# The second mixing one step later, with a third buffer of mixed blocks

## The chip, the cores and the metric

The kernel runs on one core of a Trainium2 chip. The metric is device time of one execution in microseconds; the kernel before takes 968.75 us (median of three runs, 968.42 to 970.42).

## The reference

Talking-heads attention, then a feed-forward layer. q, k, v have the shape (4, 12, 448, 64): batches, heads, positions, width of a head. The scores of all 12 heads are mixed across heads before the softmax and once more behind it:

```python
scores = scale * q @ k.T                              # per batch and head, 448 x 448
scores = einsum('bhij,hg->bgij', scores, w_pre)       # first mixing, 12 x 12
attn = exp(scores - max_j); attn = attn / (sum_j attn + 1e-9)
attn = einsum('bhij,hg->bgij', attn, w_post)          # second mixing
x = (attn @ v), heads side by side                    # 1792 x 768
out = (s * relu(x @ w_in)**2 + b) @ w_out             # 768 -> 2048 -> 768
```

## The kernel before

The attention is cut into 16 chunks (four per batch, 110 or 118 query rows each) and these into 180 blocks of 10 (or 9) query rows times 12 heads, 120 partitions by 448 keys. One loop over steps s works on several blocks at once; every engine carries out its instructions in the order in which the loop issues them (nothing reorders them later). In step s stand, in this order:

- `relayout(s+5)`: a DMA brings the scores of a block from `S` (rows by heads) to `blk` (120 partitions). `split(s+2)`, GpSimd (L559, L560): high and low part, `hl`, two buffers.
- One piece of a weight conversion for the later layer (VectorE, with one ScalarE copy `mk` in seven pieces), from step 12 (`CONV0`) until seven units are done.
- `normalize(s-1)`: reciprocal of the sum (VectorE L591) and the high half of the normalized block in fp16, `eh` (ScalarE L593), two buffers.
- `evacuate(s-3)`: copies the mixed block `po` from PSUM into the chunk's tile `A` (VectorE L631, in the last chunk ScalarE L629).
- `premix(s)`: the first mixing, three matmuls into a PSUM bank `pm` (L572; three banks in turn, `pm` twice and `px`), the maximum (VectorE L574), exp in place with its sum (ScalarE L579), the sum scaled (ScalarE L583).
- `remainder(s-1)`: low half of `eh` (VectorE L600), the last reader of the bank.
- `postmix(s-2)`: the second mixing, 12 matmuls of 120 columns with `eh` as weights, into `po` (L615; two PSUM buffers).
- What a plan has for the step: transposes of q and k (`prep_q` L460, `prep_k` L438), `av_pair` (attention times v of two heads, 16 matmuls, L513, with ScalarE copies `xs` L527), `qk_pair` (scores of two heads of a later chunk, six matmuls, L485, evacuated into `S` by ScalarE, L495). In most of the loop AV and QK pairs stand in the same steps, every second one, so heavy and light steps alternate.

The plan gives the AV pairs of chunks 0 to 13 fixed steps, the first not before the chunk's last block is evacuated (`w0 = first[ci + 1] + 3`). The pairs of chunks 14 and 15, and 18 pieces of the later layer's first product (`head_piece`, L247), are dealt out to the last steps by costs and due times; six head pieces and the AV pairs of chunk 15 come after the loop. Then three weight units are converted, `x` of the next batch is split (`xg`, L223 and L232), and the feed-forward layer runs (L247, L300) until the end.

Before the loop a tile of ones, `keep`, feeds matmuls that occupy TensorE while the first data arrive. It has a place of its own in the pool of constants. `mk` is one buffer of 1536 bytes per partition in the conversions' pool `cvp`.

Of the kernel before, what the change touches and what calls it, by code (L numbers as in the profile page):

```python
# [11 lines left out]
F16 = mybir.dt.float16  # L12
# [9 lines left out]
def talking_heads_attention__then__act_relu2_kernel(  # L22
# [14 lines left out]
    B, H, S, D = q.shape  # L37
    DM = H * D
    DFF = moe_w_in.shape[1]
    P = 128  # L40
# [7 lines left out]
    BP = BI * H  # L48
    CH = 120
    NKC = DM // P  # L50
# [11 lines left out]
    NCH = len(chunks)  # L62
# [3 lines left out]
    first = []  # L66
# [9 lines left out]
    NB = len(blocks)  # L76
# [9 lines left out]
    cvp = ctx.enter_context(tc.tile_pool(name="cvp", bufs=1))  # L86

    att = ExitStack()
    cst = att.enter_context(tc.tile_pool(name="cst", bufs=1))
    sp = att.enter_context(tc.tile_pool(name="sp", bufs=2))  # L90
    blkp = att.enter_context(tc.tile_pool(name="blkp", bufs=3))
# [90 lines left out]
    def convert_step(upto):  # L182

        if done["run"] is None:
            if done["conv"] >= min(upto, len(units)):
                return False
            done["run"] = conversion(done["conv"])
        try:
            next(done["run"])
        except StopIteration:  # L190
            done["run"] = None
            done["conv"] += 1
        return True
# [35 lines left out]
    def low_parts():  # L229
        while later:  # L230
            o, x, hi = later.pop(0)
            nc.vector.tensor_tensor(out=o, in0=x, in1=hi.bitcast(F32), op=ALU.subtract)  # L232
# [37 lines left out]
    NHEAD = 3  # L270
# [276 lines left out]
    def relayout(t):  # L547
        ci, i0, ni = blocks[t]
        blk = blkp.tile([BP, S], F32, tag="blk", name=f"blk_{t}", bufs=LD)
        nb = first[ci + 1] - first[ci]  # L550
        r = t - first[ci]
        nc.sync.dma_start(blk[:ni * H, :], s_t[ci][r:r + nb * (ni - 1) + 1:nb, :, :])
        blk_t[t] = blk

    def split(t):
        n = blocks[t][2] * H
        blk = blk_t.pop(t)
        hl = blkp.tile([BP, 2, S], F32R, tag="hl", name=f"hl_{t}", bufs=2)
        nc.gpsimd.tensor_scalar(hl[:n, 0, :], blk[:n], 1.0, 0.0, op0=ALU.mult, op1=ALU.add)  # L559
        nc.gpsimd.tensor_tensor(  # L560
            out=hl[:n, 1, :], in0=blk[:n], in1=hl[:n, 0, :].bitcast(F32), op=ALU.subtract
        )
        hl_t[t] = hl
# [23 lines left out]
    def normalize(t):  # L587

        n = blocks[t][2] * H
        e, st = e_t[t]  # L590
        nc.vector.reciprocal(st[:n, 3:4], st[:n, 2:3])  # L591
        eh = blkp.tile([BP, 2, S], F16, tag="eh", name=f"eh_{t}", bufs=2)
        nc.scalar.activation(eh[:n, 0, :], e[:n], AF.Copy, scale=st[:n, 3:4])  # L593
        eh_t[t] = eh

    def remainder(t):
        n = blocks[t][2] * H
        e, st = e_t.pop(t)
        eh = eh_t[t]
        nc.vector.scalar_tensor_tensor(  # L600
            out=eh[:n, 1, :], in0=e[:n], scalar=st[:n, 3:4], in1=eh[:n, 0, :],
            op0=ALU.mult, op1=ALU.subtract,
        )

    def postmix(t):
        ci, i0, ni = blocks[t]
        n = ni * H
        eh = eh_t.pop(t)
        if i0 == 0:
            a_t[ci] = ap_.tile([P, NC, H, CH], F32, tag="A", name=f"A_{ci}")  # L610
        po = ps.tile([P, 512], F32, tag="po", name=f"po_{t}", bufs=2)
        for c in range(NC):
            j0 = min(c * P, S - P)
            for m, (x, y) in enumerate(((1, 0), (0, 1), (0, 0))):
                nc.tensor.matmul(  # L615
                    po[:, c * BP:(c + 1) * BP],
                    eh[:n, x, j0:j0 + P],
                    wpost[:n, y].rearrange("p g i -> p (g i)"),
                    start=(m == 0),
                    stop=(m == 2),  # L620
                )
        po_t[t] = po

    def evacuate(t):
        ci, i0, ni = blocks[t]
        dst = a_t[ci][:, :, :, i0:i0 + ni]
        src = po_t.pop(t)[:, :NC * BP].rearrange("p (c g i) -> p c g i", c=NC, g=H)[:, :, :, :ni]
        if ci == NCH - 1:
            nc.scalar.activation(dst, src, AF.Copy)  # L629
        else:  # L630
            nc.vector.tensor_copy(dst, src)  # L631
# [3 lines left out]
    FILL = 1.33  # L635
    QK_COST, AV_COST = 0.8, 1.3
    LATE = 6
# [6 lines left out]
    def at(step, order, f, *args):  # L644
        plan.append((step, order, len(plan), f, args))
# [6 lines left out]
    def visits(ci):  # L652

        w0, w1 = first[ci - 1] - LD, first[ci] - LD
        return [w0 + i for i in (1, 3, 5, 7, 9, w1 - w0 - 1)]

    fill = []
    for ci in range(2, NCH):
        b, _, _ = chunks[ci]
        w0 = first[ci - 1] - LD  # L660
# [10 lines left out]
        for p, step in enumerate(visits(ci)):  # L671
            if news:
                t = w0 - back + 8 if p == 0 else w0 + 2 * p - 2
# [4 lines left out]
            load[step] = load.get(step, 0) + QK_COST  # L678
    for ci in range(NCH):
        b = chunks[ci][0]  # L680
        w0 = first[ci + 1] + 3
        if ci < NCH - 2:
            after = visits(ci + 3) if ci + 3 < NCH else [first[NCH - 1] - LD + i for i in (1, 3, 5, 7)]
            steps = [x for x in visits(ci + 2) if x >= w0] + [x for x in after if x < first[ci + 2] + 3]
            assert len(steps) == NP
            for p, step in enumerate(steps):
                at(step, 2, av_pair, ci, p)
                load[step] = load.get(step, 0) + AV_COST
                if b + 1 < B and chunks[ci + 1][0] != b:
                    at(step, 4, load_v, b + 1, p)  # L690
            continue
        w1 = first[ci + 2] + 3 if ci + 2 <= NCH else NB + 100
        if ci == NCH - 1:
            w0 = NB + 3
        for p in range(NP):
            when = w0 + p * min(w1 - w0, 12) / NP
            fill.append((when, w0, w1 - 1, AV_COST, 1, av_pair, (ci, p)))
    w0 = first[NCH - 1] - XA + 2
    for i in range(NHEAD * NKC):
        if i < NHEAD * NKC - LATE:  # L700
            when = w0 + i * (NB + 3 - w0) / (NHEAD * NKC - LATE)
            fill.append((when, w0 + i // 2, NB + 2, 0.567, 1, head_piece, ()))
        else:
            fill.append((NB + 100, NB + 3, NB + 100, 0.567, 1, head_piece, ()))
    fill.sort(key=lambda x: x[0])
    spent, closed = 0.0, {}
    for s in range(NB + 4):
        spent = max(spent, -0.4) + load.get(s, 0)
        left, held = [], set()
        for x in fill:  # L710
            _, lo, hi, cost, order, f, args = x
            waits = f in held

            opens = f is qk_pair or (f is av_pair and args[1] % 4 == 0)
            if opens and closed.get(f, -1) >= s and s <= NB + 2 and s < hi:
                waits = True

            if f is qk_pair and s in load and s < hi:
                waits = True
            if not waits and lo <= s and (s > NB + 2 or hi <= s or (x[0] < s + 4 and spent < FILL)):  # L720
                at(s, order, f, *args)
                spent += cost
                if f is qk_pair or (f is av_pair and args[1] in (3, NP - 1)):
                    closed[f] = s
            else:
                held.add(f)
                left.append(x)
        fill = left
        spent -= FILL
# [12 lines left out]
        if not early:  # L742
            state["next"] = k0

    keep = cst.tile([P, 512], F16, name="keep")
    nc.gpsimd.memset(keep, 1.0)
    make_identity(nc, ident)
    busy = ps.tile([P, 512], F32, tag="px", name="busy")
# [51 lines left out]
    while plan[0][0] < 0:  # L800
        x = plan.pop(0)
        x[3](*x[4])
        low_parts()
    tail = first[NCH - 1]
    for s in range(NB + 3):
        if s == tail - LD:
            early.close()
            rp = ctx.enter_context(tc.tile_pool(name="rp", bufs=1, side="right", reuse_waits="tile"))
            for n in range(NU_EARLY, NU_EARLY + NU_TAIL):
                w_pool[n] = rp  # L810
        if s + LD < NB:
            relayout(s + LD)
        if s + LS < NB:
            split(s + LS)
        if 0 <= s - 1 < NB:
            if s >= CONV0:
                convert_step(NU_EARLY)
            normalize(s - 1)
        if 0 <= s - 3 < NB:
            evacuate(s - 3)  # L820
        if s <= tail - XA:
            low_parts()
        if s < NB:
            premix(s)
        low_parts()
        if 0 <= s - 1 < NB:
            remainder(s - 1)
        run_plan(s, True)
        if 0 <= s - 2 < NB:
            postmix(s - 2)  # L830
        run_plan(s, False)
        if 0 <= s - (tail - LD) < NKC // 2:
            for kc in range(2):
                load_x(0, 0, 2 * (s - (tail - LD)) + kc)
        if 0 <= s - (tail - XA) < NKC:
            split_x(0, 0, s - (tail - XA))
        if 0 <= s - tail < NKC:
            load_x(0, 1, s - tail)
# [106 lines left out]
```

## Time and profile before

| | |
|---|---|
| median of three runs | 968.75 us |
| the profiled execution | 969.14 us, of which the span is 967.4 us |
| TensorE matmul / weight load busy | 928.9 us (96%) / 786.4 us (81%) |
| VectorE / ScalarE / GpSimd busy | 640.2 / 595.8 / 397.1 us |
| the block loop | premix from 30 us to 486 us |

The span runs from the first to the last instruction. PE is TensorE's matmul row, PEld its weight loads, DVE VectorE, ACT ScalarE, POOL GpSimd. The ends of matmuls are modelled and matmuls are pipelined: the start of one after the start of another tells the pace better than their lengths. An idle time in brackets is what the engine sat through before that instruction, and what released it. Names are the program's, with buffer numbers left out.

### The profile page before, as it was taken

The numbers are of one execution on the slowest core, as the hardware profiler recorded it, in microseconds if no ns is written. First come the engines' busy times: TensorE is split into PE (matmuls) and PEld (weight loads), VectorE is DVE, ScalarE is ACT, GpSimd is POOL, SyncE is SP. The second block draws the span as 40 slices with busy tenths as digits, with TensorE's granted clock in tenths as the row PEclk, the third lists the DMA queues.
The fourth block names the chain that finished last, engine by engine and source line by source line (L and its number), as shares of the span: only waits on it lengthen the run. The fifth ranks groups of instructions, "written<-read, shape, count | busy, mean of one in ns | idle before, by whom it ended". The sixth has DMA issues, their size and how long they took to land.

```text
span 967.4 us, 19864 instructions
## 1 busy us (share of the span) xinstructions
PE 928.9 (96%) x7515; PEld 786.4 (81%) x7515; DVE 640.2 (66%) x1314; ACT 595.8 (62%) x1315; POOL 397.1 (41%) x469
## 2 busy tenths in 40 slices
PE   6889999999999999999989999999999999999998
PEld 3656767777777777777779999999998999999998
DVE  4789999888878888788678217746716811849311
ACT  3587777777888888888777878422216787711000
POOL 3766667666676667666613323100001332310000
PEclk8899999999999999999999999999999999999999
DMA  4665645654455544645422302234431410237431
GB/s 103 165 152 143 173 115 147 174 135 136 122 138 145 134 129 116 154 123 160 121 70 90 123 23 84 82 115 139 147 139 42 154 59 1 69 112 215 144 99 50
DMA packets 124252, 114.63 MB, mean 118 GB/s; under 512 B 61656, under 2 KB 120044, under 8 KB 124156
## 3 DMA queue, kind: packets, MB, share of 16 engines
q1 hardware_dynamic: 114630, 101.69, 38.1%
q10 hardware_dynamic: 9366, 11.59, 3.4%
q8 instruction: 59, 0.97, 0.4%
q0 software_dynamic: 160, 0.09, 0.1%
q14 instruction: 37, 0.30, 0.1%
HBM read 58.28 MB, written 16.52 MB: 77 GB/s over the span
## 4 chain that ended last, share of the span: by engine, by line
PE 65%; ACT 14%; DVE 14%; DMA 4%; issue 2%; POOL 1%; SPq 0%; ACTq 0%; DVEq 0%; POOLq 0%
PE po L300 24%; PE ph L247 16%; PE po L615 6%; PE pm L572 5%; PE xp L513 5%; PE sc L485 5%; ACT S L495 4%; ACT pm L579 3%; DVE eh L600 3%; ACT eh L593 3%; DVE A L631 2%; DVE st L574 2%; DMA nq<-in_q_dram 1%; PE trk L438 1%; DMA blk<-S 1%
## 5 line engine op out<-in xcount | busy, mean ns | idle before, releaser
L300 PE MATMUL po<-w,g 128*128 128x384 f32 x1344 | 234.6, 336 | 2.6 <-ACT h L255 2.6
L300 PEld LDWEIGHTS po<-w,g 128*128 128x128 f32 x1344 | 233.7, 188 | 3.3 <-ACT h L255 3.2
L560 POOL TENSOR_TENSOR hl<-blk,hl 120x448 fp32r<-120x448 f32 x180 | 205.8, 1143 | 15.0
L265 POOL TENSOR_TENSOR g<-h,g 128x448 fp32r<-128x448 f32 x64 | 77.7, 1214 | 291.5 <-ACT g L264 278.2
L615 PEld LDWEIGHTS <-eh 120*128 120x128 f16 (+1 forms) x2160 | 115.8, 98 | 65.8 <-DVE eh L600 42.5
L247 PE MATMUL ph<-x,w 128*128 128x448 f32 x810 | 166.1, 364 | 0.0
L559 POOL TENSOR_SCALAR hl<-blk 120x448 fp32r<-120x448 f32 x180 | 104.5, 581 | 141.7 <-PE pm L572 124.5
L247 PEld LDWEIGHTS ph<-x,w 128*128 128x128 f32 x810 | 151.9, 188 | 12.1
L615 PE MATMUL po<-wpost,eh 120*128 120x120 f16 (+1 forms) x2160 | 145.6, 218 | 16.6 <-DVE eh L600 14.9
L579 ACT ACTIVATE pm<-pm,st 120x448 f32<-120x448 f32 x180 | 109.8, 610 | 56.4 <-DVE st L574 55.8
L600 DVE SCALAR_TENSOR_TENSOR eh<-pm,st,eh 120x448 f16<-120x448 f32 x180 | 122.1, 678 | 18.0 <-ACT eh L593 14.7
L593 ACT ACTIVATE eh<-pm,st 120x448 f16<-120x448 f32 x180 | 114.2, 634 | 18.5 <-DVE st L591 16.1
L574 DVE TENSOR_REDUCE st<-pm 120x1 f32<-120x448 f32 x180 | 111.0, 617 | 22.0 <-PE pm L572 20.5
L631 DVE COPY A<-po 128x480 f32<-128x480 f32 x168 | 106.8, 636 | 0.1
L572 PE MATMUL pm<-hl,wpre_hi 120*120 120x448 f32 x360 | 102.9, 367 | 0.7 <-POOL hl L560 0.7
L495 ACT ACTIVATE S<-sc 110x896 f32<-110x896 f32 (+1 forms) x90 | 82.5, 917 | 22.0 <-PE sc L485 17.5
L513 PE MATMUL xp<-A,v 128*64 128x110 f32 (+1 forms) x1536 | 93.7, 265 | 0.6 <-ACT A L629 0.6
L153 ACT ACTIVATE mk<-raw 128x384 f32<-128x384 f32 x64 | 35.4, 553 | 91.7 <-DMA raw<-in_moe_w_out_dram 35.0
L485 PE MATMUL sc<-Tk,Tq 64*110 64x448 f32 (+1 forms) x576 | 84.4, 400 | 5.6 <-DVE Tq L232 3.6
L513 PEld LDWEIGHTS xp<-A,v 128*64 128x64 f32 x1536 | 74.2, 136 | 10.2 <-ACT A L629 1.1
L572 PE MATMUL pm<-hl,wpre_lo 120*120 120x448 f32 x180 | 82.1, 456 | 0.0
L232 DVE TENSOR_TENSOR x<-xraw,x 128x448 fp32r<-128x448 f32 x36 | 24.1, 695 | 76.9 <-ACT x L223 76.9
(74 smaller groups left out, 999.8 us busy)
## 6 DMA issues: line engine op xcount, KB each, us to landing
blk<-S SPq DMA_DIRECT2D x172, 210.0 KB
raw<-in_moe_w_in_dram SPq DMA_DIRECT2D x32, 384.0 KB
raw<-in_moe_w_out_dram SPq DMA_DIRECT2D x32, 384.0 KB
xraw<-xd SPq DMA_DIRECT2D x48, 224.0 KB
part<-ob ACTq DMA_DIRECT2D x28, 192.0 KB
acc<-part SPq DMA_DIRECT2D x28, 192.0 KB
out_dram<-acc ACTq DMA_DIRECT2D x28, 192.0 KB
v<-in_v_dram SPq DMA_DIRECT2D x24, 192.0 KB
```

What stands on the lines that cost most here:

```text
L247: nc.tensor.matmul(ph[:, :S], w[:, i, c0:c0 + P], x[:, y, :], start=(kc == 0 and m == 0), stop=(kc == NKC - 1 and m == 2),)
L300: nc.tensor.matmul(po[:, :NO], g[:, x, c0:c0 + P], w[:, y, :], start=(f == 0 and m == 0), stop=(f == NF - 1 and m == 2),)
L485: nc.tensor.matmul(sc[e][:n, :S], qt[r0:r0 + D, p, x, :n], kt[r0:r0 + D, y, :], start=(m == 0), stop=(m == 2),)
L513: nc.tensor.matmul(xp[e * D:(e + 1) * D, p % 4, :n], vt[:, e, c, :], a[:, c, 2 * p + e, :n], start=(c == 0), stop=(c == NC - 1),)
L560: nc.gpsimd.tensor_tensor(out=hl[:n, 1, :], in0=blk[:n], in1=hl[:n, 0, :].bitcast(F32), op=ALU.subtract)
L572: nc.tensor.matmul(pm[:n, :S], w[:n, :n], hl[:n, x, :], start=(m == 0), stop=(m == 2))
L574: nc.vector.tensor_reduce(out=st[:n, 0:1], in_=pm[:n, :S], axis=AX.X, op=ALU.max, negate=True)
L579: nc.scalar.activation(e[:n], e[:n], AF.Exp, bias=st[:n, 0:1], accum_out=pm[:n, S:S + 1])
L593: nc.scalar.activation(eh[:n, 0, :], e[:n], AF.Copy, scale=st[:n, 3:4])
L600: nc.vector.scalar_tensor_tensor(out=eh[:n, 1, :], in0=e[:n], scalar=st[:n, 3:4], in1=eh[:n, 0, :], op0=ALU.mult, op1=ALU.subtract,)
L615: nc.tensor.matmul(po[:, c * BP:(c + 1) * BP], eh[:n, x, j0:j0 + P], wpost[:n, y].rearrange("p g i -> p (g i)"), start=(m == 0), stop=(m = ...
L631: nc.vector.tensor_copy(dst, src)
```

## The change

`postmix` runs three steps behind `premix` and `evacuate` four; `eh` has three buffers; the loop and the plan's bounds are one step longer. `keep` becomes the first tile with the tag `mk` in `cvp`, as 768 fp16 values of which 512 are used. The rest of the program is the same text. By the plan's own arithmetic the AV pairs of chunks 0 to 13 stay in their steps; from step 170 on AV pairs of chunk 14 and head pieces are dealt out anew (the last pair of chunk 14 goes from step 178 to 179).

```diff
--- before.py
+++ after.py
@@ -589,7 +589,7 @@
         n = blocks[t][2] * H
         e, st = e_t[t]
         nc.vector.reciprocal(st[:n, 3:4], st[:n, 2:3])
-        eh = blkp.tile([BP, 2, S], F16, tag="eh", name=f"eh_{t}", bufs=2)
+        eh = blkp.tile([BP, 2, S], F16, tag="eh", name=f"eh_{t}", bufs=3)
         nc.scalar.activation(eh[:n, 0, :], e[:n], AF.Copy, scale=st[:n, 3:4])
         eh_t[t] = eh
 
@@ -678,10 +678,10 @@
             load[step] = load.get(step, 0) + QK_COST
     for ci in range(NCH):
         b = chunks[ci][0]
-        w0 = first[ci + 1] + 3
+        w0 = first[ci + 1] + 4
         if ci < NCH - 2:
             after = visits(ci + 3) if ci + 3 < NCH else [first[NCH - 1] - LD + i for i in (1, 3, 5, 7)]
-            steps = [x for x in visits(ci + 2) if x >= w0] + [x for x in after if x < first[ci + 2] + 3]
+            steps = [x for x in visits(ci + 2) if x >= w0] + [x for x in after if x < first[ci + 2] + 4]
             assert len(steps) == NP
             for p, step in enumerate(steps):
                 at(step, 2, av_pair, ci, p)
@@ -689,22 +689,22 @@
                 if b + 1 < B and chunks[ci + 1][0] != b:
                     at(step, 4, load_v, b + 1, p)
             continue
-        w1 = first[ci + 2] + 3 if ci + 2 <= NCH else NB + 100
+        w1 = first[ci + 2] + 4 if ci + 2 <= NCH else NB + 100
         if ci == NCH - 1:
-            w0 = NB + 3
+            w0 = NB + 4
         for p in range(NP):
             when = w0 + p * min(w1 - w0, 12) / NP
             fill.append((when, w0, w1 - 1, AV_COST, 1, av_pair, (ci, p)))
     w0 = first[NCH - 1] - XA + 2
     for i in range(NHEAD * NKC):
         if i < NHEAD * NKC - LATE:
-            when = w0 + i * (NB + 3 - w0) / (NHEAD * NKC - LATE)
-            fill.append((when, w0 + i // 2, NB + 2, 0.567, 1, head_piece, ()))
+            when = w0 + i * (NB + 4 - w0) / (NHEAD * NKC - LATE)
+            fill.append((when, w0 + i // 2, NB + 3, 0.567, 1, head_piece, ()))
         else:
-            fill.append((NB + 100, NB + 3, NB + 100, 0.567, 1, head_piece, ()))
+            fill.append((NB + 100, NB + 4, NB + 100, 0.567, 1, head_piece, ()))
     fill.sort(key=lambda x: x[0])
     spent, closed = 0.0, {}
-    for s in range(NB + 4):
+    for s in range(NB + 5):
         spent = max(spent, -0.4) + load.get(s, 0)
         left, held = [], set()
         for x in fill:
@@ -712,12 +712,12 @@
             waits = f in held
 
             opens = f is qk_pair or (f is av_pair and args[1] % 4 == 0)
-            if opens and closed.get(f, -1) >= s and s <= NB + 2 and s < hi:
+            if opens and closed.get(f, -1) >= s and s <= NB + 3 and s < hi:
                 waits = True
 
             if f is qk_pair and s in load and s < hi:
                 waits = True
-            if not waits and lo <= s and (s > NB + 2 or hi <= s or (x[0] < s + 4 and spent < FILL)):
+            if not waits and lo <= s and (s > NB + 3 or hi <= s or (x[0] < s + 4 and spent < FILL)):
                 at(s, order, f, *args)
                 spent += cost
                 if f is qk_pair or (f is av_pair and args[1] in (3, NP - 1)):
@@ -742,7 +742,7 @@
         if not early:
             state["next"] = k0
 
-    keep = cst.tile([P, 512], F16, name="keep")
+    keep = cvp.tile([P, 6 * P], F16, tag="mk", name="keep")[:, :512]
     nc.gpsimd.memset(keep, 1.0)
     make_identity(nc, ident)
     busy = ps.tile([P, 512], F32, tag="px", name="busy")
@@ -802,7 +802,7 @@
         x[3](*x[4])
         low_parts()
     tail = first[NCH - 1]
-    for s in range(NB + 3):
+    for s in range(NB + 4):
         if s == tail - LD:
             early.close()
             rp = ctx.enter_context(tc.tile_pool(name="rp", bufs=1, side="right", reuse_waits="tile"))
@@ -816,8 +816,8 @@
             if s >= CONV0:
                 convert_step(NU_EARLY)
             normalize(s - 1)
-        if 0 <= s - 3 < NB:
-            evacuate(s - 3)
+        if 0 <= s - 4 < NB:
+            evacuate(s - 4)
         if s <= tail - XA:
             low_parts()
         if s < NB:
@@ -826,8 +826,8 @@
         if 0 <= s - 1 < NB:
             remainder(s - 1)
         run_plan(s, True)
-        if 0 <= s - 2 < NB:
-            postmix(s - 2)
+        if 0 <= s - 3 < NB:
+            postmix(s - 3)
         run_plan(s, False)
         if 0 <= s - (tail - LD) < NKC // 2:
             for kc in range(2):
```

## Rows read from the trace of the kernel before

**Rows 1.** Busy us by stretch: PE, PEld, DVE, ACT, POOL; clock, DMA share, GB/s.
```profile
75.00:190.00 115.00, 109.65 (x1203) 80.25 (x1202) 105.75 (x231) 91.17 (x229) 76.45 (x93) 1.00 0.56 149
190.00:460.00 270.00, 263.55 (x2949) 195.58 (x2948) 221.32 (x458) 216.84 (x539) 182.85 (x226) 1.00 0.51 137
```

**Rows 2.** Waits, whole trace: engine line <- releaser: us, times, longest.
```profile
PEld L615 <- DVE eh L600: 42.5, 76, 1.8
...
PE po L615 <- DVE eh L600: 14.9, 38, 1.4
...
PEld L615 <- issue: 10.5, 47, 0.2
...
PEld trq L460 <- ACT S L495: 2.9, 8, 0.7
```

**Rows 3.** Waits of TensorE's weight loads in 28:75, 75:190, 190:460, 460:492 us.
```profile
PEld L615 <- DVE eh L600: 9.5, 11, 1.8
...
PEld L615 <- DVE eh L600: 10.0, 18, 1.3
...
PEld L615 <- DVE eh L600: 20.2, 43, 0.9
...
PEld L615 <- DVE eh L600: 2.8, 4, 1.3
```

**Rows 4.** Waits of VectorE in 28:75, 75:190 and 190:460 us.
```profile
DVE st L574 <- PE pm L572: 0.5, 1, 0.5
...
DVE st L574 <- PE pm L572: 1.1, 3, 0.5
...
DVE st L574 <- PE pm L572: 13.0, 30, 0.9
```

**Rows 5.** Timeline, 250 to 257 us: start, length, engine, line [idle before <- releaser].
```profile
250.33 0.61 DVE L574 TENSOR_REDUCE st<-pm 120x1 f32<-120x448 f32 x1
...
251.77 0.80 PE L615 MATMUL po<-wpost,eh 120*128 120x120 f16 x12 [0.28 <-DVE eh L600]
...
252.51 0.97 PE L513 MATMUL xp<-A,v 128*64 128x110 f32 x16
252.52 0.61 DVE L574 TENSOR_REDUCE st<-pm 120x1 f32<-120x448 f32 x1
...
253.05 0.68 DVE L600 SCALAR_TENSOR_TENSOR eh<-pm,st,eh 120x448 f16<-120x448 f32 x1
253.17 0.61 ACT L579 ACTIVATE pm<-pm,st 120x448 f32<-120x448 f32 x1 [0.39 <-DVE st L574]
...
253.88 0.17 ACT L583 ACTIVATE st<-pm 120x1 f32<-120x1 f32 x1
...
254.20 0.47 PE L572 MATMUL pm<-hl,wpre_lo 120*120 120x448 f32 x1
...
254.31 0.92 ACT L495 ACTIVATE S<-sc 110x896 f32<-110x896 f32 x1 [0.27 <-PE sc L485]
...
254.91 0.80 PE L615 MATMUL po<-wpost,eh 120*128 120x120 f16 x12
255.10 0.62 DVE L574 TENSOR_REDUCE st<-pm 120x1 f32<-120x448 f32 x1 [0.30 <-PE pm L572]
255.13 0.62 ACT L593 ACTIVATE eh<-pm,st 120x448 f16<-120x448 f32 x1
...
255.52 0.43 PE L572 MATMUL pm<-hl,wpre_lo 108*108 108x448 f32 x1
...
255.76 0.61 ACT L579 ACTIVATE pm<-pm,st 120x448 f32<-120x448 f32 x1
255.79 0.68 DVE L600 SCALAR_TENSOR_TENSOR eh<-pm,st,eh 120x448 f16<-120x448 f32 x1
...
256.53 0.65 PE L615 MATMUL po<-wpost,eh 120*128 120x120 f16 x9 [0.17 <-DVE eh L600]
```

**Rows 6.** Timeline, the last second mixing.
```profile
489.71 0.80 PE L615 MATMUL po<-wpost,eh 108*128 108x120 f16 x12 [1.15 <-DVE eh L600]
```

## The prediction

> **What bounds the kernel now.** I read the busy shares by stretch first, then the waits, then one piece of the timeline. Between 190 and 460 us, where nothing but the block loop runs, TensorE shows 263.6 of 270 us busy at the full granted clock (1.00 of 2.4 GHz); between 75 and 190, where VectorE also has the weight conversions, VectorE shows 105.8 of 115 [rows 1]. So TensorE looks full, with VectorE close behind. Who waits for whom says more: the second mixing (L615) is held up by the remainder `eh` (L600, VectorE) 76 times, 42.5 us on the weight-load row and 14.9 us on the matmul row [rows 2]. Neither figure is the delay. On the weight-load row an idle of 10.5/47 = 0.22 us stands even before a second mixing that had only to be issued, so the delay is 42.5 - 76 x 0.22 = 25.8 us. On the matmul row most of it is hidden behind the modelled end of the premix matmul before.
>
> The timeline shows one delay [rows 5]. In the even step the second mixing starts 0.71 us after its premix (254.20, 254.91). In the next it starts 1.01 us after (255.52, 256.53), because `eh` of that block is written from 255.79 to 256.47. That is 0.30 us lost, in a pair of steps of 4.76 us (251.77 to 256.53). Without it TensorE's own work in the pair is 4.46 us.
>
> By stretch the same subtraction gives [rows 3]: 28 to 75 us, 9.5 - 11 x 0.22 = 7.1; 75 to 190, 10.0 - 18 x 0.22 = 6.0; 190 to 460, 20.2 - 43 x 0.22 = 10.7; 460 to 492, 2.8 - 4 x 0.22 = 1.9. That is all the change can take away: 25.7 us.
>
> **The change part by part.** *Second mixing three steps behind, a third `eh`.* No instruction is added or removed: 180 times 12 matmuls, one VectorE or ScalarE copy each, as before; no DMA moves, SP and POOL get the same order. In the loop `postmix(s-3)` now needs a remainder issued two steps earlier, so the 0.30 us wait should go. The third buffer keeps `normalize` one step behind the reader of its buffer, as two did at distance two, so no wait arises there. What is late next has to be asked of each resource:
>
> - *Premix and its PSUM bank.* A bank comes back after three blocks, once its remainder has read it. The remainder that starts at 253.05 ends at 253.73; the premix into that bank starts at 255.52 [rows 5]: 1.8 us of slack against the 0.30 us by which TensorE comes earlier.
> - *The chain of VectorE and ScalarE.* One block's maximum, exp, sum, reciprocal, copy of `A` and the next block's maximum follow each other. With no wait for TensorE they take 252.52 - 250.33 = 2.19 us [rows 5]. In a step in which ScalarE also evacuates scores (S, L495), exp follows exp by way of S and `eh`: the sum's line starts at 253.88 and ends at 254.05, S could start then instead of 254.31, `eh` comes 0.82 after S (255.13) and exp 0.63 after that (255.76), so at the earliest at 255.50, 2.33 us after 253.17. A pair of steps is thus 2.19 + 2.33 = 4.52 us, a little more than TensorE's 4.46. So this chain takes over, and the pair falls from 4.76 to 4.52: 0.24 of the 0.30 us is won, 80%.
>
> From that, by stretch:
>
> - 190 to 460 us: 80% of 10.7 is 8.6. The chain is not yet the limit here: VectorE's maximum waits for the premix 13.0 us in all [rows 4]. From it I take something off for the transposes of q, which wait for S to leave its bank already now (8 times, 2.9 us in the whole trace [rows 2]). A chunk of 11 or 12 blocks has two, so some 20 stand in this stretch, and a TensorE that arrives earlier may wait there: 0 to 20 x 0.25 = 5 us. There is no row for it; I take 0.1 each, 2 us, nearer to nothing since few wait today. Left: 6.6.
> - 75 to 190 us: TensorE loses 6.0, but the maximum waits for TensorE only 1.1 us in all [rows 4]; VectorE is the limit, and TensorE will be late somewhere else. Bounds 0 and 6.0; I take 1.5, near the 1.1.
> - 28 to 75 us: TensorE has little other work in the first steps and the maximum waits 0.5 us for it [rows 4]. Bounds 0 and 7.1; I take 0.8.
> - 460 to 492 us: VectorE is less loaded, and the last second mixing alone waits 1.15 us on the matmul row [rows 6]. The loop is one step longer, but what TensorE does before that last mixing is the same: one more second mixing (0.61) and the last `av_pair` of chunk 14 now lie behind the last premix and fill the wait. Against that, its `xs` copies now stand ahead of the last `normalize` on ScalarE. Bounds -1 and 1.9; I take 1.2.
>
> *First AV pair of a chunk.* The last copy of `A` moves one step later; by the plan's arithmetic the AV pairs of chunks 0 to 13 stay in the very steps they have now. Slack goes from two steps to one. Today's lag covers it (rival C); cost 0, at most as worked there. *Plan of the last chunk.* AV pairs and head pieces shift by a step or two; TensorE's sum is the same: 0. *Tile of ones.* `keep` is written and read before the loop; the first conversion that reuses its scratch comes in step 12. 0; hidden by twelve steps.
>
> Sum: 6.6 + 1.5 + 0.8 + 1.2 = 10.1 us off the profiled execution's 969.14: 959.0. The span is 967.4, the 1.7 us around it stay. The median of before is 968.75, 0.4 lower, so 958.6; I say 958.5.
>
> Two views of TensorE differ widely on the room there is. Rows 1 show its matmuls 97.6% busy between 190 and 460 us, its weight loads 72.4%. The Trainium skill, Perfetto Trace Analysis, section Identifying the Most-Contended Engine, says that matmul busy time tells headroom badly and weight-load busy time better. By the one there would be at most 6.4 us to win in that stretch, by the other an estimated 74; start-to-start times give 10.7, so here the first view is the nearer one, though too low.
>
> **Rivals.** *A, the wait moves.* Premix waits for a PSUM bank or TensorE for S instead, and the chain gives nothing beyond what it has: of 10.7 only a quarter, 2.7, and 0.8 at the start. 969.14 - 3.5, on the median 965.2. For it: 4.52 against 4.76 is a small margin, taken from one pair of steps. Against: 13.0 us in which the maximum waits for the premix. The Trainium skill, Perfetto Trace Analysis, Optimization Strategy under Identifying Performance Opportunities, reads a gap that keeps repeating as a possible lack of SBUF or PSUM buffers; here that would be PSUM, which gets none. The trace names a late producer and 1.8 us of bank slack, so it speaks against.
>
> *B, all comes back.* TensorE alone is the limit outside the start: 10.7 + 6.0 + 1.9 + 0.8 = 19.4, so 949.4. For it: 97.6% busy in rows 1. Against: VectorE's 92% before 190 us.
>
> *C, slower: the first AV pair of each chunk waits for the last copy.* From the premix of the step before, AV starts 0.71 + 0.61 + 0.71 + 0.74 = 2.77 us later [rows 5], where 0.74 is 251.77 to 252.51. The copy ends when that step's maximum starts. That is now 0.90 us after its premix in the even step (254.20, 255.10) and 0.90 - 1.32 + 2.19 = 1.77 in the other. If TensorE used the whole new step, 2.23, as lead, the lag would be 4.00 and each of 14 pairs would wait 1.23: 17.2 us, and 969.14 - 10.1 + 17.2 gives a median of 975.8. It eats the gain from a lag of 2.77 + 10.1/14 = 3.5 us on. Against: a premix cannot pass the remainder three blocks back, which ends 1.2 us after the maximum of the block behind it (252.52, 253.73). AV follows its own step's premix by 1.45, so it comes 2.66 us after a maximum whose successor, and the copy before that, is due after 2.2 to 2.3.
>
> **How the numbers follow.** The forecast's case (954 to 963.5) 0.60; A 0.17; B 0.12; nothing measurable, since the start and the conversions limit more than I read, 0.05; C 0.06. Under 0.2% (1.9 us) a measurement of this kernel cannot tell from no change. Faster: 0.60 + 0.12 + A but for 0.01, 0.88; within 0.2%: 0.06; slower: 0.06. The range runs from between B and the forecast, 951.5, to 967, which takes in A: some 2 in 10 lie outside.
>
> **What would show it.** Right: the wait of L615 for `eh` is nearly gone between 190 and 460 us and the pair of steps takes about 4.5 us; the maximum's wait for the premix shrinks below 13.0; the stretch before 190 us hardly shortens. Wrong: premix waits for L600 (A), pairs at 4.46 us and conversions faster too (B), L513 waiting for L631 at the start of chunks (C).

## The result, and the profile after

The changed kernel takes 959.67 us (median of 4 runs, 959.31 to 960.51) against 969.37 us of the kernel before in the same comparison: ratio 0.9908 [0.9893, 0.9922], 9.7 us faster. Its profiled execution took 959.49 us with a span of 957.8, 9.6 less than before. The forecast was 958.5.

The waits of the whole trace (engine, line <- releaser: us, times, longest), to be held against [rows 2]; of the second mixing (L615) waiting for `eh` (L600) no row is left:

```profile
PEld L615 <- issue: 40.2, 181, 0.3
...
DVE st L591 <- ACT st L583: 29.7, 94, 0.9
...
DVE eh L600 <- ACT eh L593: 22.3, 49, 0.8
...
PEld trq L460 <- ACT S L495: 12.4, 18, 1.6
...
PE trq L460 <- ACT S L495: 9.3, 15, 1.5
DVE st L574 <- PE pm L572: 9.2, 15, 0.9
...
ACT eh L593 <- PE po L615: 2.6, 9, 0.3
...
PE pm L572 <- DVE eh L600: 2.1, 4, 1.0
```

40.2/181 is 0.22 us, the idle that stands before any second mixing: the whole delay of 25.7 us is gone, and the kernel got 9.7 of it. Part of the rest shows in the other rows. TensorE now waits before the transposes of q (`trq`, L460) until ScalarE has copied `S` out of the bank: 12.4 us in 18 waits on the weight-load row, where [rows 2] had 2.9 in 8. Less 0.22 each that is 8.4 us against 1.1, so 7.3 of the 16 us that were removed and not won stand there. VectorE's maximum (L574) waits little for the premix any more, 9.2 us in all where [rows 4] had 13.0 behind 190 us alone. Its remainder waits longer for ScalarE's `eh` (L600 for L593: 22.3 us, 14.7 before); the wait of L591 for L583 is about what it was (29.7 us, 31.0 before). By stretch (75 to 190 us first, then 190 to 450), where the block loop now ends some 10 us earlier:

```profile
PE trq L460 <- ACT S L495: 4.2, 6, 1.5
...
DVE st L574 <- PE pm L572: 1.3, 3, 0.5
...
DVE st L574 <- PE pm L572: 5.2, 7, 0.9
...
PE trq L460 <- ACT S L495: 2.2, 7, 0.5
```

The busy times of the same stretches, columns as in [rows 1]: TensorE at 98.9% of 260 us where it had 97.6%, so this view alone would say that there is nothing left to win.

```profile
75.00:190.00 115.00, 109.20 (x1216) 81.25 (x1217) 105.49 (x233) 92.22 (x231) 77.53 (x95) 1.00 0.58 152
190.00:450.00 260.00, 257.26 (x2914) 193.34 (x2913) 214.92 (x452) 210.82 (x532) 181.57 (x224) 1.00 0.52 137
```

A pair of steps in the timeline (start, length, engine, line; idle before it in brackets), answering to [rows 5]:

```profile
250.96 0.61 ACT L579 ACTIVATE pm<-pm,st 120x448 f32<-120x448 f32 x1 [0.39 <-DVE st L574]
...
251.55 0.47 PE L572 MATMUL pm<-hl,wpre_lo 120*120 120x448 f32 x1
...
251.97 0.92 ACT L495 ACTIVATE S<-sc 110x896 f32<-110x896 f32 x1
...
252.27 0.80 PE L615 MATMUL po<-wpost,eh 120*128 120x120 f16 x12
...
252.88 0.43 PE L572 MATMUL pm<-hl,wpre_lo 108*108 108x448 f32 x1
...
253.29 0.61 ACT L579 ACTIVATE pm<-pm,st 120x448 f32<-120x448 f32 x1
...
253.56 0.81 PE L615 MATMUL po<-wpost,eh 120*128 120x120 f16 x12
...
254.20 0.16 DVE L591 RECIPROCAL st<-st 120x1 f32<-120x1 f32 x1
...
254.46 0.63 ACT L593 ACTIVATE eh<-pm,st 120x448 f16<-120x448 f32 x1 [0.29 <-PE po L615]
254.84 0.61 DVE L574 TENSOR_REDUCE st<-pm 108x1 f32<-108x448 f32 x1
...
255.48 0.61 ACT L579 ACTIVATE pm<-pm,st 108x448 f32<-108x448 f32 x1 [0.39 <-DVE st L574]
...
255.99 0.45 PE L572 MATMUL pm<-hl,wpre_lo 108*108 108x448 f32 x1
```

Both second mixings start 0.7 us behind their premix with nothing to wait for. From exp to exp it is 2.33 us across the step with `S` (250.96, 253.29) and 2.19 across the other (253.29, 255.48): 4.52 together, the chain as it was worked out. The premix, though, follows at 4.44 (251.55, 255.99), which is TensorE's own pace: in this pair TensorE does not wait for the chain. One pair is not the pace of the stretch either: between blocks 60 and 170 the 55 pairs take 4.94 us each on average, 5.07 before, since transposes and other work stand between them.

How the gain is spread: the last maximum of each of the four batches, before and then after. The first maximum starts at 31.26 us before and at 32.24 after. The last line of the second list is the first product behind the loop that needs the new `xg`; it is used below.

```profile
143.39 0.61 DVE L574 TENSOR_REDUCE st<-pm 108x1 f32<-108x448 f32 x1
...
259.85 0.62 DVE L574 TENSOR_REDUCE st<-pm 108x1 f32<-108x448 f32 x1 [0.27 <-PE pm L572]
...
373.52 0.62 DVE L574 TENSOR_REDUCE st<-pm 108x1 f32<-108x448 f32 x1 [0.28 <-PE pm L572]
...
486.48 0.62 DVE L574 TENSOR_REDUCE st<-pm 108x1 f32<-108x448 f32 x1 [0.61 <-PE pm L572]
```

```profile
143.06 0.61 DVE L574 TENSOR_REDUCE st<-pm 108x1 f32<-108x448 f32 x1
...
257.02 0.61 DVE L574 TENSOR_REDUCE st<-pm 108x1 f32<-108x448 f32 x1
...
369.00 0.61 DVE L574 TENSOR_REDUCE st<-pm 108x1 f32<-108x448 f32 x1
...
476.54 0.62 DVE L574 TENSOR_REDUCE st<-pm 108x1 f32<-108x448 f32 x1 [0.20 <-PE pm L572]
...
491.56 3.87 PE L247 MATMUL ph<-xg,w 128*128 128x448 f32 x18 [0.97 <-DVE xg L232]
```

Batch by batch the loop is 1.3, 2.5, 1.7 and 5.4 us shorter (first maximum to 143.06, then the differences). The last second mixing no longer waits the 1.15 us of [rows 6].

Batches are cut otherwise than the stretches of the prediction. The maxima of the same two blocks, 60 and 170 counted from 0, near 190 and 460 us, before and then after:

```profile
185.42 0.62 DVE L574 TENSOR_REDUCE st<-pm 120x1 f32<-120x448 f32 x1
...
463.98 0.61 DVE L574 TENSOR_REDUCE st<-pm 120x1 f32<-120x448 f32 x1
```

```profile
184.13 0.61 DVE L574 TENSOR_REDUCE st<-pm 120x1 f32<-120x448 f32 x1
...
456.05 0.61 DVE L574 TENSOR_REDUCE st<-pm 120x1 f32<-120x448 f32 x1
```

From the one to the other it is 278.6 us before and 271.9 after.

### The profile page after: what moved, and what is told of

Its sections match the earlier page's. It is cut to its first block, busy times and chain, and to the rows that moved or that the text cites. A ratio compares the mean times of both kernels' runs of the same rounds, so it can differ in the third digit from the quotient of the medians.

```text
span 957.8 us, 19990 instructions
## 1 busy us (share of the span) xinstructions
PE 923.6 (96%) x7515; PEld 787.1 (82%) x7515; DVE 635.1 (66%) x1314; ACT 592.4 (62%) x1315; POOL 398.7 (42%) x469
## 4 chain that ended last, share of the span: by engine, by line
PE 64%; ACT 15%; DVE 13%; DMA 4%; issue 2%; POOL 2%; SPq 1%; ACTq 0%; DVEq 0%; POOLq 0%
PE po L300 24%; PE ph L247 17%; PE pm L572 7%; PE po L615 5%; PE xp L513 5%; PE sc L485 5%; ACT S L495 4%; ACT pm L579 4%; DVE A L631 2%; ACT eh L593 2%; DVE st L574 2%; PE trk L438 1%; DVE eh L600 1%; DMA blk<-S 1%; ACT xs L527 1%
## 5 line engine op out<-in xcount | busy, mean ns | idle before, releaser
L615 PEld LDWEIGHTS <-eh 120*128 120x128 f16 (+1 forms) x2160 | 115.5, 98 | 40.5 <-issue 40.2
L615 PE MATMUL po<-wpost,eh 120*128 120x120 f16 (+1 forms) x2160 | 144.5, 217 | 0.6 <-ACT A L629 0.2
L600 DVE SCALAR_TENSOR_TENSOR eh<-pm,st,eh 120x448 f16<-120x448 f32 x180 | 122.2, 679 | 25.2 <-ACT eh L593 22.3
L593 ACT ACTIVATE eh<-pm,st 120x448 f16<-120x448 f32 x180 | 114.3, 635 | 16.6 <-DVE st L591 13.2
L574 DVE TENSOR_REDUCE st<-pm 120x1 f32<-120x448 f32 x180 | 110.6, 614 | 10.2 <-PE pm L572 9.2
L631 DVE COPY A<-po 128x480 f32<-128x480 f32 x168 | 106.7, 635 | 0.0
L495 ACT ACTIVATE S<-sc 110x896 f32<-110x896 f32 (+1 forms) x90 | 82.4, 915 | 19.6 <-PE sc L485 15.7
L153 ACT ACTIVATE mk<-raw 128x384 f32<-128x384 f32 x64 | 35.5, 554 | 94.1 <-DMA raw<-in_moe_w_out_dram 40.7
```

Source lines behind the costliest of these rows:

```text
L574: nc.vector.tensor_reduce(out=st[:n, 0:1], in_=pm[:n, :S], axis=AX.X, op=ALU.max, negate=True)
L600: nc.vector.scalar_tensor_tensor(out=eh[:n, 1, :], in0=e[:n], scalar=st[:n, 3:4], in1=eh[:n, 0, :], op0=ALU.mult, op1=ALU.subtract,)
L615: nc.tensor.matmul(po[:, c * BP:(c + 1) * BP], eh[:n, x, j0:j0 + P], wpost[:n, y].rearrange("p g i -> p (g i)"), start=(m == 0), stop=(m = ...
```

## The experiments

Each was timed beside the kernel before; a ratio is to that kernel, with its 95% interval in brackets.

**The third buffer and the tile of ones alone**, at the old distance:

```diff
-        eh = blkp.tile([BP, 2, S], F16, tag="eh", name=f"eh_{t}", bufs=2)
+        eh = blkp.tile([BP, 2, S], F16, tag="eh", name=f"eh_{t}", bufs=3)
...
-    keep = cst.tile([P, 512], F16, name="keep")
+    keep = cvp.tile([P, 6 * P], F16, tag="mk", name="keep")[:, :512]
```

> Three eh buffers and the tile of ones in the conversion's scratch, but the second mixing still two steps behind. My theory (the distance is what removes the wait): same as before, 968.5 to 970, and the wait of L615 for eh stays at about 42 us on the weight-load row. Rival (the third buffer, or the place of the tiles in memory, is what counts): about 960, as the changed kernel.

967.73 us, 0.9989 [0.9976, 1.0002], just under the range of my theory and far from the rival's. Its wait is that of before: 41.9 us in 75 on the weight-load row, and on the matmul row, as in [rows 2]:

```profile
PE po L615 <- DVE eh L600: 14.9, 40, 1.4
```

So the buffer and the place of the tile win nothing that shows by themselves, and the distance is what wins.

**The new distance with the plan of before** for the last chunks (every `+ 4` of the plan back to `+ 3`):

> The changed kernel with the plan of before for the last chunks (AV pairs of chunk 14 and the head pieces dealt out as before, chunk 15 after step 183). My theory (distance alone): 959 to 960.5, as the changed kernel; the last premix comes about 1 us later and the end of the loop does not. Rival (a good part of the 5.4 us won in the last batch comes from dealing the last steps out anew): 961.5 to 963.

967.94 us, 0.9986 [0.9975, 0.9998]: all was lost again, against every expectation. Most of it was lost behind the loop: from the last second mixing (481.3 us, one behind after's) to the end it is 485.1 us, 477.4 in after. My edit also brought the AV pairs of chunk 15 and the six late head pieces into the loop's last step, where neither kernel has them, so the copies `xs` (L527) stand on ScalarE ahead of the `mk` copy of the conversions (L153), and wait there for the AV products. The timeline:

```profile
486.21 0.81 ACT L527 ACTIVATE xs<-xp,xscale 128x400 f32<-128x400 f32 x2 [3.55 <-PE xp L513]
...
488.32 0.55 ACT L153 ACTIVATE mk<-raw 128x384 f32<-128x384 f32 x1
...
488.90 0.36 DVE L162 TENSOR_SCALAR raw<-raw 128x384 uint32<-128x384 uint32 x1 [7.18 <-ACT mk L153]
...
498.28 1.08 PE L247 MATMUL ph<-xg,w 128*128 128x448 f32 x2 [6.70 <-DVE xg L232]
```

VectorE sat 7.18 us, the conversions and the split of `x` came late, and TensorE waited 6.70 us for `xg` where after's waits 0.97. So I ran it again with chunk 15 and the late head pieces left behind the loop, as after has them; only chunk 14 and twelve head pieces go back to their old steps:

```diff
-        w0 = first[ci + 1] + 4
+        w0 = first[ci + 1] + 3
...
-        w1 = first[ci + 2] + 4 if ci + 2 <= NCH else NB + 100
+        w1 = first[ci + 2] + 3 if ci + 2 <= NCH else NB + 100
...
-            when = w0 + i * (NB + 4 - w0) / (NHEAD * NKC - LATE)
-            fill.append((when, w0 + i // 2, NB + 3, 0.567, 1, head_piece, ()))
+            when = w0 + i * (NB + 3 - w0) / (NHEAD * NKC - LATE)
+            fill.append((when, w0 + i // 2, NB + 2, 0.567, 1, head_piece, ()))
...
```

> As e2, but with the AV pairs of chunk 15 and the last head pieces left behind the loop and the conversions, so that ScalarE's order there is that of the changed kernel; only chunk 14's pairs and twelve head pieces stand in the steps of before. My theory (the distance wins, the new order of the last steps little): within 1 us of the changed kernel, the 6.7 us wait before xg gone. Rival (the new order of the last steps is worth 2 us or more): 961.5 to 963.

960.92 us, 0.9925 [0.9909, 0.9941]: 1.1 us above the second timing of after (959.81, below), and the intervals overlap. The new deal of the last steps is thus worth little, 1 us by the medians, and 2 us is not excluded. The profile agrees: from the maximum of block 170 to the last second mixing it is 25.6 us here, 25.7 before and 24.3 after, so what is won at the end of the loop hangs on the new deal. The pair of runs shows one thing more, that keeping chunk 15 and the late head pieces behind the loop is worth 6 (by the ratios) to 7 us (by the medians).

**Without the transposes of q.** Chunks 4 to 15 take the transposed q of chunk 2 or 3; their loads, transposes and copies are left out, in both kernels alike:

```diff
+    def same_q(ci):
+        q_t[ci] = q_t[2 + ci % 2]
...
-            at(step, 1, prep_q, ci, half)
+            at(step, 1, *((prep_q, ci, half) if ci < 4 else (same_q, ci)))
-        at(min(starts) - 8, 0, load_q, ci)
+        if ci < 4:
+            at(min(starts) - 8, 0, load_q, ci)
```

> The changed kernel without the transposes of q of chunks 4 to 15 (24 halves: loads, transposes, copies, low parts); their scores are those of the q of chunks 2 and 3. It takes some 10 us of TensorE's and 12 to 13 us of VectorE's and ScalarE's work away and with it TensorE's wait for S before L460 (9.3 us in the changed kernel). My theory (that wait is where part of the removed one went): 946 to 949. The same edit on the kernel before follows and tells the two apart: there 959 to 961, so the distance is worth 12 to 14 us without those transposes. Rival (the moved wait only shows a limit that stands elsewhere): the distance is worth the same 9 to 10 us.

> The kernel before with the edit of e3 (no transposes of q for chunks 4 to 15). My theory (part of the removed wait moved to those transposes): 961 to 963, so that the distance is worth 12 to 14 us without them. Rival (the moved wait is only where a limit shows that stands elsewhere): 958 to 960, so that it is worth the same 9 to 10 us.

After without them 949.20 us, 0.9801 [0.9787, 0.9814]; before without them 964.94 us, 0.9959 [0.9947, 0.9971]. The distance is then worth 15.7 us, more than the 12 to 14 that I expected; the changed kernel lies at the edge of its range, the kernel before above both of its own. It gains only some 4 us from the edit, and waits more for `eh` instead (line 618 here is 615 there):

```profile
PEld L618 <- DVE eh L603: 49.1, 74, 1.8
```

The changed kernel gains 10.6 us (959.81 in its second timing below). Its wait for `S`:

```profile
PE trq L460 <- ACT S L498: 4.9, 3, 2.0
```

It falls from 9.3 to 4.9 us with the transposes gone. The 6 us that the distance is worth more are not all given back by the transposes, though. Without them there is also more to remove: 49.1 - 74 x 0.22 = 32.8 us, 7 more than the 25.8 with them. What is removed and not won is 17 us without the transposes and 16 with them. All 6 us come between blocks 60 and 170, where the distance wins 13.1 us instead of 6.7. How much of that is TensorE's wait for `S`, and how much the transposes' own work on TensorE, VectorE and ScalarE, this edit cannot separate, since it takes all of them away.

**The conversions spread over the loop**, one piece every third step; if VectorE bounds the time before 190 us alone, this moves its work to where it has room:

```diff
-            if s >= CONV0:
+            if s >= CONV0 and s % 3 == 0:
```

> The changed kernel with a conversion piece in every third step from step 12 on instead of in each of 49 successive steps. My theory (between 75 and 190 us VectorE with the conversions is the limit, so the distance gave little there): 955 to 957.5, nearly all of it won before 200 us, a little given back after. Rival (there TensorE, or its waits for S, is the limit): 959 to 960.5.

> The kernel before with the same spread. My theory: the conversions hold VectorE back less, but the second mixing two steps behind keeps its 0.3 us waits and gets new ones after 200 us, so only 1 to 3 us are won: 966.5 to 968.5, and the distance is then worth 11 to 12 us instead of 9.7. Rival (spread and distance simply add): 964 to 966, the same 3 to 4 us as on the changed kernel.

After with it 958.67 us, 0.9896 [0.9881, 0.9911]. After itself, timed again with the second run of the plan of before:

> The changed kernel once more, to have it on the same chip as the next three: 959 to 960.5, ratio to before 0.990 to 0.992.

959.81 us, 0.9904 [0.989, 0.9918]. Before with it 969.85 us, 1.0009 [1.0, 1.0019]. Nothing that shows is won in either kernel, and both expectations missed: the first is between its two ranges, the second above both. The maxima of the changed kernel with the pieces spread (first one at 29.68 us):

```profile
136.86 0.61 DVE L574 TENSOR_REDUCE st<-pm 108x1 f32<-108x448 f32 x1
...
474.95 0.62 DVE L574 TENSOR_REDUCE st<-pm 108x1 f32<-108x448 f32 x1 [0.20 <-PE pm L572]
```

Batch one is 107.2 us from its first maximum, where after has 110.8; by the end it is 445.3 against 444.3. What is won early is given back where the pieces now stand: by the maxima of the same blocks, blocks 20 to 60 take 101.3 us instead of 104.5, and blocks 60 to 170 take 277.4 instead of 271.9. So before 190 us the pieces did hold the loop back, as I had read, and behind it VectorE has less room for them than the busy share (214.92 of 260) seemed to show.

**One link of the chain taken out.** The sum is no longer scaled by ScalarE (L583); the reciprocal reads it from PSUM, and the factor goes into the scale of `x`. The 1e-9 added to the sum goes with it.

```diff
+    totals = {}
...
-        total = pm[:, S:S + 1]
-        nc.scalar.activation(
-            st[:n, 2:3], total[:n], AF.Copy, scale=2.0 ** -15, bias=1e-9 * 2.0 ** -15
-        )
+        totals[t] = pm[:, S:S + 1]
...
-        nc.vector.reciprocal(st[:n, 3:4], st[:n, 2:3])
+        nc.vector.reciprocal(st[:n, 3:4], totals[t][:n])
...
-        nc.vector.tensor_scalar_mul(xscale, mx[:, 2:3], 2.0 ** -29)
+        nc.vector.tensor_scalar_mul(xscale, mx[:, 2:3], 2.0 ** -14)
```

> The changed kernel without L583: the reciprocal reads the sum in PSUM itself, the factor 2**-15 moves into xscale. It takes about 0.2 us out of each step's chain of VectorE and ScalarE and leaves TensorE's work as it is. My theory (after the change that chain, not TensorE, sets the pace of most steps): 4 to 8 us less than the changed kernel, 952 to 956; pairs that took 4.52 us go to TensorE's 4.46. Rival (TensorE and its waits for S set the pace): within 1 us of the changed kernel.

> The kernel before with the edit of e5 (no L583, a chain shorter by 0.2 us). My theory (two steps behind, TensorE waits for a remainder that comes 0.06 to 0.3 us late; a chain shorter by 0.2 to 0.4 us by then removes most of that, but unevenly): 956 to 960, the wait of L615 for eh on the weight-load row falls from 42 us to 15 to 25, and the distance is worth 4 to 8 us on top. Rival (distance and chain are independent and add): 960.5 to 962, the distance worth its 9 to 10 us here too.

After with it 952.03 us, 0.9823 [0.981, 0.9836]: 7.8 us less than after, for an instruction of 0.17 us, and for the hop to it from engine to engine, that only VectorE was seen to wait for. The pair of steps in its timeline (line 573 is the premix, 575 the maximum):

```profile
241.77 0.46 PE L573 MATMUL pm<-hl,wpre_lo 120*120 120x448 f32 x1
...
246.22 0.47 PE L573 MATMUL pm<-hl,wpre_lo 120*120 120x448 f32 x1
...
247.14 0.62 DVE L575 TENSOR_REDUCE st<-pm 120x1 f32<-120x448 f32 x1 [0.38 <-PE pm L573]
```

4.45 us a pair (and 4.45 in the next), which is TensorE's own 4.46; and VectorE waits for TensorE again:

```profile
DVE st L575 <- PE pm L573: 31.1, 59, 1.7
```

31.1 us where after has 9.2: VectorE has got room. But behind 190 us, where most of that wait stands (24.5 us), the loop did not get faster for it. The maxima of blocks 60 and 170:

```profile
176.97 0.61 DVE L575 TENSOR_REDUCE st<-pm 120x1 f32<-120x448 f32 x1
...
448.75 0.61 DVE L575 TENSOR_REDUCE st<-pm 120x1 f32<-120x448 f32 x1
```

That is 271.8 us, and after takes 271.9, in both of its profiles. The link wins its time earlier: from the first maximum to block 60 it is 146.7 us, where two profiles of after have 151.9 and 153.3. So the chain holds the loop back in the first 60 blocks, where the conversion pieces stand in it too, and behind them a chain that is shorter changes nothing. My theory forecast the time rightly and the place wrongly; behind 190 us the rival was right.

Before with it takes 960.97 us, 0.9912 [0.9899, 0.9925], slower than my theory and inside the rival's range. Its second mixing still waits for `eh`, longer than the 15 to 25 us that I expected:

```profile
PEld L613 <- DVE eh L598: 34.6, 68, 1.3
```

The distance gives 8.9 us on top of the shorter chain, as it gives 9.7 without it: the two edits add. By the stretches they act mostly in different places, the shorter chain before block 60, the distance behind it; in the kernel before, the shorter chain also takes 2.7 us off blocks 60 to 170 (278.6 to 275.9), and the wait for `eh` falls from 42.5 to 34.6 us.

**Both, the shorter chain and the spread conversions:**

> e5 on the changed kernel, with the conversion pieces in every third step as in e4. After e5 VectorE waits for TensorE again (31 us), so that it has room behind 190 us for pieces that cost their time there in e4. My theory: 948 to 950.5, the 4 us that e4 won before step 60 stay. Rival (a piece costs the same wherever it stands): 951 to 953, as e5.

951.95 us, 0.9824 [0.9804, 0.9843], by the median the same as the shorter chain alone and in the rival's range. The four runs lie between 949.35 and 954.38, so a gain of 2 us is not excluded; the fastest is the one profiled, and there blocks 20 to 60 take 100.0 us (102.2 with the shorter chain alone) and blocks 60 to 170 take 272.3 (271.8). So with the shorter chain the moved pieces cost 0.5 us behind block 60, where they cost 5.5 without it. Apart from the run without the transposes, these two are the fastest versions, 17 us under the kernel before.

## Why the prediction was right

*The removable delay*, 25.7 us by the starts of L615 less 0.22 each: right, all of it went, and more than half was not won. The idle of the weight-load row as it stands, 42.5 us, would have said four times the gain, the matmul row's 14.9 half as much again.

*The chain takes over at 4.52, so 80% is won*: the chain does take 4.52 where it was looked at, in the parts 2.33 and 2.19, but it does not set the pace behind 190 us. A chain shortened by a link leaves blocks 60 to 170 at 271.8 us against 271.9, and the premix of the pair shown follows at TensorE's own 4.44. Added up over the starts of TensorE's work in these 110 blocks, what stands between premix and second mixing fell from 56.4 to 45.1 us, 11.3 us, and what stands before the 17 transposes of q grew from 11.9 to 15.2. So the delay was removed whole, and 3.3 of the 4.7 us that were removed there and not won stand before the transposes. That TensorE's own work sets the pace otherwise fits its 98.9% and these starts, but no run changes that work alone.

*The terms by stretch.* By the starts of the maxima of blocks 20, 60 and 170 (from 0) and of the last second mixing: 28 to 75 us, priced 0.8, cannot be told: the stretch takes 48.3 us from the first maximum before, 47.4 and 48.8 in two profiles after. Of the 7.1 us removed there nothing shows as won; in their place stand the premix's waits for L600 (2.1 us) and 3.2 us on the weight-load row before transposes of q, where it was 0.6. 75 to 190, priced 1.5: 105.8 to 104.5, 1.4 before rounding. 190 to 460, priced 6.6: 278.6 to 271.9, 6.6 before rounding. The end, priced 1.2: 25.7 to 24.3, 1.5 before rounding. That the sum agrees this closely is partly luck. In the largest term I took off 2.1 us for the chain, which costs nothing there that shows, and 2 us for the transposes of q, before which the starts show 3.3 more; the two errors nearly cancel. The wait for `S` grew by more ahead of 190 us, where I priced none.

*The stretch before 190 us* I put down to VectorE's conversions. That is shown: with the pieces moved out blocks 20 to 60 take 101.3 us, with a shorter chain 102.2, with both 100.0, where after takes 104.5.

*No wait for the third buffer*: nearly. `eh` (L593) waits 9 times, 2.6 us, for the second mixing that reads its buffer. In the pair shown, at 254.46, its reciprocal had ended only at 254.36, so some 0.1 us is lost. The remainder behind it starts at 255.37, when the next maximum (254.84, 0.61 long) is all but done, and the next exp at 255.48 waits for that maximum, not for `eh`: off the chain.

*The rivals.* A (the wait moves to the PSUM bank, or to TensorE waiting for `S`): the bank hardly, since the premix waits for L600 4 times, 2.1 us in all, every time before 75 us; `S` in part, with 7.3 us, though not to the degree of A, since 9.7 us were won. B (all comes back): its sign, pairs at 4.46, shows behind 190 us, but of 11.3 us removed there 6.6 came, since the transposes wait, and before 190 us VectorE's conversions held the loop. C: no AV pair waits for L631; the copy comes in time. The tile of ones at 0: the first run shows no effect. The redeal at 0: about 1 us by the third run, at the end of the loop; the term of the end had counted on the `av_pair` that it moves.

The two views of headroom: the matmul row's 6.4 us in 190 to 460 stands beside 6.6 won there. With the link taken out TensorE keeps its own 4.46 with the weight-load row busy for 195.79 of 260 us. The Trainium skill, Perfetto Trace Analysis, Identifying the Most-Contended Engine, judges TensorE's headroom not by matmul busy time but by MFU (the share of the peak arithmetic that is done) and by weight-load busy time. For the weight loads these figures do not bear that out.

## What to carry to other kernels

Price a wait by the start-to-start times around it less the idle that stands there even without a wait, and then ask of each resource what will be late next. That the next chain is a little longer than TensorE's own work in one pair did not make it the limit; a run that shortens the chain tells, and it has to be read by stretch. Between the same two blocks 271.9 us stayed 271.8, while the time of the whole (7.8 us less) and the waits of VectorE (9.2 to 31.1) both seemed to say that the limit had moved there. Where VectorE had the conversions as well, busy for 105.49 of 115 us, the small link won most of its 7.8 us. When work is moved, look at what it comes to stand ahead of in the queue of another engine, as the copies of chunk 15 did.

## What the runs showed of the hardware

TensorE's clock after an idle stretch. In the first run with the plan of before TensorE did nothing from 491.6 to 498.3 us; the windows (columns as in [rows 1]):

```profile
494.00:498.00 4.00, 0.00 (x0) 0.00 (x0) 3.77 (x9) 3.61 (x8) 0.00 (x0) 0.50 0.32 98
498.00:502.00 4.00, 3.72 (x10) 3.36 (x11) 3.96 (x8) 3.84 (x7) 1.75 (x1) 0.50 0.32 98
502.00:506.00 4.00, 4.00 (x17) 3.58 (x17) 0.96 (x2) 3.38 (x7) 2.08 (x3) 0.78 0.00 0
506.00:512.00 6.00, 6.00 (x31) 5.45 (x30) 5.76 (x12) 4.72 (x9) 1.89 (x2) 1.00 0.23 70
```

The granted clock fell to 0.50 (1.2 GHz) and stayed there for the first matmuls behind the idle; from 506 us on it was 1.00 (2.4 GHz) again. The first ten matmuls behind the wait took 3.87 us from start to start, 2.10 in after, where the clock was 1.00. The product behind the wait started 6.7 us later than after's, and the span ended 8.6 later (966.4, 957.8); the slower matmuls account for about that difference of 1.9 us. The first maximum starts at 29.6 to 32.2 us in the profiles of kernels with the same start, so a gain of 1 us there cannot be read off one profile.
